# Nineteen loads on Pool's queue in joined packets, and an order table redrawn to match: a chunk-select attention with a gated feed-forward on one Trainium2 core

## The chip, the cores and the metric

The kernel runs on one core of one Trainium2 chip. The metric is the device time of one execution in microseconds (us). The profile comes from one profiled execution; its span is the time from the first to the last recorded instruction of the core. The engines are named as in the profile: PE is the matmul engine, DVE the vector engine, ACT the scalar engine, POOL is GpSimd, SP is the engine that does nothing here but issue DMAs.

## The reference

```python
B, H, S, D = 4, 8, 768, 64              # q, k, v
k_chunks = k.reshape(B, H, 24, 32, D)
k_min, k_max = min(k_chunks, axis=3), max(k_chunks, axis=3)
ub = sum(maximum(q * k_min, q * k_max), axis=-1)   # a bound for each query and chunk of 32 keys
ub = where(chunk is not later than the query's, ub, -1e9)
top_chunks = argsort(ub)[..., -6:]
scores = where(key's chunk in top_chunks and key <= query, q @ k.T / 8, -1e9)
attn = softmax(scores)
x = (attn @ v).transpose(0, 2, 1, 3).reshape(3072, 512)
gate = sigmoid(x @ w_gate)              # 512 -> 1536
return (gate * (x @ w_val)) @ w_out     # 1536 -> 512
```

All inputs and the output are float32.

## The kernel before

**Units.** The 3072 tokens are cut into blocks of 128 (six to a batch) and the blocks into eight units of up to 384 tokens: u0 holds the first blocks of batches 0, 1 and 2, whose queries see only their own block and so need no choice of chunks; u1 holds blocks 1 to 3 of batch 0; u2 blocks 4 and 5 of batch 0 and the first block of batch 3; u3 to u7 follow through batches 1 to 3. For each unit: queries and keys are transposed (kT, qT, kt, qf), chunk minima and maxima are made (kx0, kx1, in `L561`), the bounds are multiplied out on PE (ub), the six best are found (mx, ap, apt on DVE), queries and keys are laid out in halves with the mask of chosen chunks as extra rows (hq, hk, hqm; copies of `L346` on Pool or `L342` on ACT), scores (sc) go by PE to PSUM, ACT exponentiates (exp, `L859`), Pool masks diagonal blocks (cm, `L865`), PE multiplies by the values (pv, `L881`), DVE divides (rz, x), PE transposes (xps) and the feed-forward follows: g and v (`L931`), sigmoid by tanh on ACT, hg on DVE (`L943`), o (`L962`), a copy to SBUF (osb) and a store (out). Units 0 to 3 run it plainly; u4 with u5 and u6 with u7 run it in pairs, by a scheme with seven products for eight.

**Loads.** `load_first` loads a batch's first block: keys kf0_b and kf1_b and queries qf0_b and qf1_b (128 KB each, rows of 256 bytes) and values vf_b (256 KB). `load_wide` loads keys and queries of u1 and u2 by pairs of heads (k0_u1 to q3_u2; 192 and 128 KB). `load_v` loads the values of one block (v_b_i, 256 KB, rows of 256 bytes). `load_blocks` (`L537`) loads the keys and queries of batches 1 to 3 in four quarters each (k00_b, k01_b, k10_b, k11_b; 384 KB each, rows of 128 bytes). `weights` and `weights_out` load w_gate, w_val and w_out in three parts each (wg, wv, wo, 512 KB), by Pool's queue. All else but one store is issued by SP. The casts of batch 1's keys to half precision (k16_1_0 to k16_1_3) each need all four quarters.

**Order.** Nothing is scheduled at run time, nor by a planner at build time. The table `ORDER` (lines 94 to 270) holds 1893 words, one for each operation of the plan, in the order of emission. A word is the operation's name, after a colon the numbers of the buffer slots that it takes, and after an @ the engine, where that isn't the first of those that the operation allows. Each engine runs its operations in the order of the table and waits where one of them isn't ready. A slot whose old contents are still needed makes its next writer wait too: scores and gate products rotate through eight PSUM slots, batch loads through two large slots ("big") and values through six ("v").

```python
def load_v(b, ib, prio):
    t = raw_v[b, ib] = Buf("v", f"v_{b}_{ib}", [128, H, D])
    plan.add(f"v_{b}_{ib}", {SP: (450, 450)}, lambda e: nc.sync.dma_start(
        at(t), v[b, :, 128 * ib:128 * ib + 128].rearrange("h p d -> p h d")),
        writes=[t], prio=prio, dma=(1150, 256))
```

The pair of numbers after an engine and the `dma` values are costs from which the table was drawn elsewhere; they don't act when the kernel is built.

Of the kernel before, what the change touches and what calls it, by code (L numbers as in the profile page):

```python
# [94 lines left out]
tri0 ap1 ident epat0:0 ident16 tri k2_u1:0 kn_u1_2:0 kT_u1_2:0 kt_u1_2:0 q1_u2:1 vf1_1:1 epat kcr0 kx0_u1_2  # L95
qn_u2_1@DVE:2 k1_u2 k3_u1 kf1_0:0 q0_u1 qn_u1_0@DVE:3 qT_u1_0:1 qf_u1_0@DVE:0 kx1_u1_2:0 k1_u1 kn_u1_3:4 hkp001@ACT
kT_u1_3:2 q2_u2 hkp010@ACT qf0_0:1 qn_u2_2:5 hkp100@ACT q2_u1 qT_u2_1:3 scm_0:4,5 hkp101@POOL kn_u1_1@POOL:6 kT_u1_1:6
kt_u1_3:1 kx0_u1_3 kx1_u1_1 hq0 hkp000 k0_u1 kn_u1_0@POOL:0 kT_u1_0:7 kt_u1_0@DVE:2 q1_u1 qn_u1_1@POOL:3 qf0_1:2
hq1_u1_0 qf_u2_1:1 hq0_u2_1@POOL qT_u1_1:0 qf1_0 kf0_0 qf_u1_1@DVE q3_u1 kf1_2:3 kfT_0:1 kf16_0@DVE:4 hk0_u1_3@ACT
hk1_u1_3@ACT kx1_u1_3 kx0_u1_1 qfT_0:3 qn_u1_2:2 qf16_0:6 kt_u1_1:1 hk0_u1_2@POOL hkp110@POOL qT_u2_2:0 qn_u1_3@POOL:0  # L100
qT_u1_3:2 qf_u1_3 kn_u2_1:3 vf_1:4 vc_1 qT_u1_2:3 hkf1 hk1_u1_1@POOL hkf0@DVE kx0_u1_0 qm_u1_1:0 kx1_u1_0 kf0_2 qf1_1
kf1_1:5 kfT_2:6 kf0_1 qf0_3:0 qf_u1_2 qm_u1_3@ACT hk0_u1_1@ACT qf1_2:1 qf0_2 hk0_u1_0@POOL vf_2:4 qf_u2_2 vf_0:3 kfT_1:2
kxf1:1 scf_0:1 kf16_2:5 expf_0_0 qfT_1:3 kf16_1@DVE:0 kcr1 kxf0 hkp011 qfT_2:7 scm_1:0,2 qm_u1_0@POOL qf16_1:2 scf_1:2
qm_u1_2@ACT kcr_u1@POOL v10 qf16_2:4 v16_0_0 expf_1_1:3 expf_1_0 hkp111@ACT q3_u2 kcr_f ub_u1:6,4 ubn0_u1:0 ubm0_u1
kf1_3:5 ubn1_u1 k2_u2 qf1_3 pvf_1_1:1 pvf_0_0:3 kT_u2_1:7 mx0_u1:0 pvf_1_0:2 ap0_u1 qfT_3:0 rzf_0_0:0 k0_u2 wg0
hq1_u1_2@POOL wv0 apt0_u1:0 rzf_1_1:1 xf_0_0:0 hk1_u1_0@ACT kn_u2_2:6 qf16_3:0 hq0_u1_1 expf_0_1:1 kT_u2_2:6 kx0_u2_2
hq0_u1_0@POOL vf1_2:2 k3_u2 hq0_u1_2@POOL scm_2:4,0 scf_2:2 expf_2_1:0 hqm0_u1_0 vc_2 xpsf_0_0:5,0 xf_1_1:1 rzf_1_0:0
pvf_0_1:3 rzf_0_1:1 qn_u2_3@POOL:3 xf_1_0:2 q0_u2 sc_u1_0_1:0,1 hqm0_u1_2 expf_2_0 vf1_3:1 xpsf_1_1:1 xTf_1_1 pvf_2_0:4
qn_u2_0:6 xTf_0_0@ACT xpsf_1_0:2 rzf_2_0:0 xTf_1_0 xf_2_0:0 qT_u2_0:5 qf_u2_0@DVE kt_u2_2@DVE:1 kx1_u2_1:0
kn_u2_0@POOL:4 hq0_u1_3@POOL hq1_u1_3@POOL kt_u2_1@DVE:2 hk1_u1_2@POOL qm_u2_1@ACT:0 exp_u1_0_1 sc_u1_1_2:1,3 xpsf_2_0:4  # L110
exp_u1_1_2 xTf_2_0@ACT qT_u2_3:0 qf_u2_3 sc_u1_1_0:2 pvf_2_1:1 rzf_2_1:0 sc_u1_0_0:5 exp_u1_1_0 sc_u1_2_2:4,2 xf_2_1:1
hk1_u2_2@POOL exp_u1_2_2 xf_0_1:2 sc_u1_3_1:0,0 exp_u1_3_1 sc_u1_3_2:2 sc_u1_2_0:4 xpsf_2_1:1 sc_u1_3_0:0 exp_u1_0_0
exp_u1_3_0 v_0_2:2 kf0_3 hk0_u2_2@ACT xTf_2_1 qm_u2_2 ubm1_u1 kx1_u2_2 kn_u2_3@POOL:5 hk0_u2_1@POOL v16_0_2 xpsf_0_1:3
kT_u2_3:5 v_0_3:1 v_0_1:3 wg1 xTf_0_1 sc_u1_0_2:1 ap0 kT_u2_0:0 sc_u1_2_1:6 sc_u1_1_1:3 exp_u1_2_0 exp_u1_1_1 kx0_u2_1
wv1 cm_u1_1 v16_0_1 kx0_u2_0 v16_0_3 exp_u1_2_1 g_u0_0:4,0,0 exp_u1_0_2 tanh_u0_0 kfT_3:7 v_u0_0:3 mx1_u1 kx0_u2_3
ap1_u1 apt1_u1 exp_u1_3_2 kf16_3:6 kt_u2_3@DVE:0 g_u0_1:6,1,1 qm_u2_0@ACT tanh_u0_1 v_u0_1:1 vf_3:0 g_u0_2:4,2,2
v_u0_2:2 hqm1_u1_0@ACT qm_u2_3@ACT hq1_u1_1 pv_u1_1:7 kx1_u2_3 cm_u1_0 pv_u1_0 tanh_u0_2 hq1 sc_u1_4_1:5,3 k11_1:0
hqm1_u1_2 cm_u1_3 exp_u1_4_1 hk1_u2_3@ACT sc_u1_7_0:6,1 g_u0_3:4,3,3 sc_u1_7_2:5 exp_u1_7_0 exp_u1_7_2 wo2 hg_u0_0
hg_u0_1 rz_u1_0:0 x_u1_0:0 kx1_u2_0 cm_u1_2 sc_u1_4_0:3 hg_u0_2 pv_u1_3:1 sc_u1_7_1:7 pv_u1_2 sc_u1_6_2:2,0
sc_u1_5_1:6,2 hq0_u2_3@POOL k01_1 kt_u2_0@DVE:1 rz_u1_1:1 tanh_u0_3 sc_u1_4_2:0 cm_u1_7 kcr_u2@POOL wg2 exp_u1_4_2  # L120
sc_u1_5_2:5 v_u0_3:4 sc_u1_5_0:0 exp_u1_7_1 exp_u1_6_2 exp_u1_5_2 exp_u1_4_0 x_u1_1:1 g_u0_4:1,0,4 sc_u1_6_1:7 ub_u2:2,5
hg_u0_3 xps_u1_0:4,1 ubn0_u2:0 cm_u1_4 wv2 ubn1_u2 mx0_u2:0 ap0_u2 apt0_u2:0 hqm0_u2_2@DVE mx1_u2 pv_u1_4:3 exp_u1_5_0
v_u0_4:0 g_u0_5:2,1,5 wo0 hq0_u2_2@POOL cm_u1_5 vc_3 k00_1 k10_1 hk0_u2_3@ACT exp_u1_6_1 exp_u1_5_1 xT_u1_0@ACT
tanh_u0_4 hg_u0_4 tanh_u0_5 scf_3:7,6,3 pv_u1_7:5 sc_u1_6_0:4 exp_u1_6_0 cm_u1_6 v_u0_5:1 hg_u0_5 g_u0_6:2,2,6 expf_3_0
tanh_u0_6 v_u0_6:4 sc_u2_2_1:7,1 pv_u1_5 xps_u1_1:2 exp_u2_2_1 sc_u2_3_1:0,2 pv_u1_6 exp_u2_3_1 hk0_u2_0@POOL hqm0_u2_0
cmf_3_0 wo1 hg_u0_6 g_u0_7:1,3,7 rz_u1_3:0 sc_u2_2_2:7 sc_u2_2_0:4 expf_3_1:0 tanh_u0_7 exp_u2_2_2 rz_u1_2:1 x_u1_3:2
pvf_3_0:0 v_u0_7:5 g_u0_8:6,0,8 x_u1_2:0 rzf_3_0:0 xf_3_0:1 sc_u2_1_1:1,3 tanh_u0_8 sc_u2_3_0:3 exp_u2_3_0 xps_u1_2:7
exp_u2_2_0 hq0_u2_0 cmf_3_1 v_u0_8:0 g_u0_9:6,1,9 tanh_u0_9 v_u0_9:3 hk1_u2_0@POOL ap1_u2 xT_u1_1 hg_u0_8 cm_u2_3
g_u0_10:2,2,10 v_u0_10:4 hq1_u2_1 g_u0_11:0,0,11 v_u0_11:6 xT_u1_2 tanh_u0_10 xpsf_3_0:7,0 hg_u0_7 apt1_u2 hg_u0_9
pvf_3_1:5 rzf_3_1:1 hg_u0_10 tanh_u0_11 sc_u2_0_2:3,0 o0_u0_0:2,0 exp_u2_0_2 sc_u2_0_1:0 o1_u0_0 hq1_u2_3@POOL  # L130
xTf_3_0@ACT hg_u0_11 xps_u1_3:4 sc_u2_1_0:3 exp_u2_1_0 hqm1_u2_0@ACT hqm1_u2_2@ACT k16_1_0:3 o2_u0_0 o0_u0_1:7,1
xT_u1_3@ACT sc_u2_3_2:6 exp_u2_3_2 o1_u0_1 xf_3_1:0 osb_u0_0@DVE hq1_u2_0@DVE o2_u0_1 hq1_u2_2 hk1_u2_1@POOL osb_u0_1
v_0_4:4 exp_u2_0_1 out_u0_0 xpsf_3_1:3 kx0_1_0 xTf_3_1 cm_u2_1 v16_0_4 sc_u2_1_2:2 sc_u2_0_0:5 exp_u2_0_0 exp_u2_1_2
exp_u2_1_1 o0_u0_2:4,0 o1_u0_2 cm_u2_0 o2_u0_2 g_u1_0:6,3,12 osb_u0_2 tanh_u1_0 v_0_5:2 v16_0_5 cm_u2_2 kx0_1_3
pv_u2_2:3 kx1_1_3:1 kx1_1_0 sc_u2_6_2:7,1 pv_u2_1:0 pv_u2_3 sc_u2_7_0:5,3 kx1_1_2 kx0_1_2 sc_u2_7_2:2 sc_u2_5_0:1,2
exp_u2_7_0 k16_1_2@DVE:2 rz_u2_1:0 pv_u2_0 rz_u2_0:1 x_u2_1:1 exp_u2_6_2 sc_u2_4_2:4,0 exp_u2_7_2 exp_u2_4_2 x_u2_0:2
k16_1_1:5 kt_1_2:4 v11 q01_1:1 v_u1_0:6 g_u1_1:5,1,13 q11_1 k16_1_3@DVE:0 hg_u1_0 sc_u2_4_0:7 exp_u2_5_0 sc_u2_6_0:3
exp_u2_6_0 v_u1_1:2 xps_u2_1:0 xps_u2_0:4 g_u1_2:1,2,14 exp_u2_4_0 xT_u2_1@ACT q10_1 kx0_1_1 kx1_1_1 hk0_1_2 cm_u2_5
cm_u2_7 tanh_u1_2 tanh_u1_1 xT_u2_0@ACT hg_u1_1 v_u1_2:3 sc_u2_5_2:6 sc_u2_6_1:7 sc_u2_7_1:0 hg_u1_2 exp_u2_5_2 kt_1_0:6
sc_u2_5_1:1 exp_u2_6_1 exp_u2_7_1 g_u1_3:5,0,15 sc_u2_4_1:4 v_u1_3:2 g_u1_4:6,3,16 tanh_u1_3 cm_u2_4 exp_u2_5_1  # L140
tanh_u1_4 cm_u2_6 kcr_1@POOL hk0_1_0 q00_1 qf0_u3_2:0 qf0_u3_1 qf0_u3_3 hq0_u3_2@POOL qm_u3_2@ACT:0 v_u1_4:3
g_u1_5:7,1,17 v_u1_5:0 v_1_3:5 v_1_4:3 v_1_0:1 v16_1_3 v16_1_0 g_u1_6:5,2,0 qf0_u3_0 kt_1_1:1 hk1_1_1 qf0_u4_3:1
qm_u3_0@ACT tanh_u1_6 ub_u3:1,6 kt_1_3:2 hg_u1_3 exp_u2_4_1 tanh_u1_5 hq1_u3_2@POOL hk0_1_1 v_u1_6:5 g_u1_7:4,0,1
pv_u2_6:2 tanh_u1_7 hk1_1_2@ACT hg_u1_4 ubn0_u3:0 qf0_u4_1 ubm0_u3 pv_u2_5:7 mx0_u3:0 hg_u1_5 ap0_u3 qf0_u4_2 hk1_1_3
hg_u1_6 apt0_u3:0 hqm0_u3_0@DVE v_u1_7:3 g_u1_8:1,3,2 v_u1_8:4 hq0_u3_0@ACT tanh_u1_8 pv_u2_7 hg_u1_7 ubn1_u3
g_u1_9:0,1,3 qf0_u4_0 sc_u3_0_1:5,1 sc_u3_1_0:1,2 sc_u3_0_2:3 pv_u2_4 sc_u3_1_2:6 tanh_u1_9 hqm0_u3_2 rz_u2_3:0 ubm1_u3
v_1_1:0 out_u0_2 exp_u3_1_0 exp_u3_0_2 exp_u3_0_1 x_u2_3:0 v_u1_9:0 v16_1_1 v16_1_4 g_u1_10:1,2,4 v_u1_10:2 sc_u3_0_0:3
tanh_u1_10 g_u1_11:5,0,5 rz_u2_2:1 hg_u1_8 k01_2:0 v_1_2:4 k00_2 k11_2 k10_2 hg_u1_9 xps_u2_3:4 x_u2_2:1 sc_u3_2_0:0,3
xps_u2_2:7 sc_u3_1_1:1 q10_2:1 out_u0_1 mx1_u3 ap1_u3 apt1_u3 xT_u2_3 kx1_2_1:0 exp_u3_0_0 exp_u3_1_2 kx1_2_0 v_u1_11:3
# [1072 lines left out]
```

## Time and profile before

| | |
|---|---|
| median of 3 runs | 287.46 us (287.25 to 287.63) |
| the profiled execution | 287.56 us |
| its span | 285.8 us |
| granted clock of PE (mean) | 0.998 |
| PE busy | 268.1 us, 94% |
| DVE busy | 230.8 us, 81% |
| ACT busy | 213.2 us, 75% |
| POOL busy | 120.7 us, 42% |
| packets of SP's and ACT's loads and stores (q1, with q10) | 118592, 27.54 MB |
| packets of Pool's queue (q0) | 4752, 4.72 MB |

Busy time says how long an engine had work in hand, and an engine with idle time may still set the end if the idle time lies where others wait for it. The slices of the page are fortieths of the span, 7.1 us each, and a digit is the busy share in tenths. A row of groups gives line, engine and operation, out<-in, the count, then busy time, the mean of one in ns, and after the second bar the idle time in front with what ended it. A row of DMA issues gives the size and the median time from issue to landing.

### The profile page before, as it was taken

The page shows a single profiled execution, that of the slowest core. Times are in us where ns is not written, and L with a number is a line of the kernel's source. Part 1 is how long each engine was busy: PE and PEld are TensorE (multiplying, and loading weights), DVE is VectorE, ACT ScalarE, POOL GpSimd, SP SyncE. Part 2 cuts the span into 40 slices and gives each one's busy share as a digit, 9 for nine tenths or more (in the row PEclk, how much of TensorE's full clock was granted, in tenths as well). Part 3 has the DMA queues.
Part 4 walks back from the last instruction along what each step waited for, and adds up shares of the span by engine and source line. Part 5 has one row for each costly group of instructions (what it writes and reads, how often), then busy time and mean ns, then how long its engine had stood idle before and what let it go on. Part 6 is the DMA issues. An engine that isn't in the chain of part 4 may idle for free.

```text
span 285.8 us, 7062 instructions
## 1 busy us (share of the span) xinstructions
PE 268.1 (94%) x2626; PEld 170.8 (60%) x2626; DVE 230.8 (81%) x626; ACT 213.2 (75%) x452; POOL 120.7 (42%) x199
## 2 busy tenths in 40 slices
PE   1677899999999899999999999999999999999995
...
DMA  6999999999999999998031000100000020100005
GB/s 167 278 225 204 208 209 209 212 174 197 181 214 148 212 214 214 217 181 149 30 85 74 4 2 0 39 37 2 38 3 2 0 110 2 73 37 3 0 17 204
DMA packets 123377, 32.69 MB, mean 114 GB/s; under 512 B 111440, under 2 KB 120400, under 8 KB 123344
## 3 DMA queue, kind: packets, MB, share of 16 engines
...
q0 software_dynamic: 4752, 4.72, 10.2%
q8 instruction: 20, 0.33, 0.5%
...
q10 hardware_dynamic: 144, 0.07, 0.1%
...
## 4 chain that ended last, share of the span: by engine, by line
PE 74%; DMA 5%; SPq 4%; DVE 3%; ACT 3%; issue 1%; POOL 0%; DVEq 0%
PE o_u L962 19%; PE sc_u L848 10%; PE v_u L931 8%; PE g_u L931 8%; PE pv_u L881 6%; SPq L537 3%; PE sug_u6u L1041 3%; PE suv_u6u L1041 3%; PE sug_u4u L1041 3%; PE suv_u4u L1041 3%; DMA k<-in_k_dram 2%; DMA q<-in_q_dram 2%; PE ube_u L787 2%; PE xps_u L908 1%; PE srv_u6u L1041 1%; PE srg_u6u L1041 1%
## 5 line engine op out<-in xcount | busy, mean ns | idle before, releaser
L859 ACT ACTIVATE att_u<-sc_u 128x512 f16<-128x512 f32 (+3 forms) x184 | 91.4, 556 | 16.2 <-PE sc_u L848 15.0
L962 PE MATMUL o_u<-wo,hg_u 128*128 128x512 f16 x216 | 52.8, 379 | 0.0
L865 POOL TENSOR_SCALAR_AFFINE_SELECT att_u<-att_u 128x384 f16<-128x384 f16 (+1 forms) x56 | 29.1, 529 | 48.7 <-ACT att_u L859 45.8
L931 PE MATMUL v_u<-xT_u,wv 128*128 128x384 f16 x192 | 39.1, 326 | 0.0
L931 PE MATMUL g_u<-xT_u,wg 128*128 128x384 f16 x192 | 39.0, 326 | 0.0
L962 PEld LDWEIGHTS <-hg_u 128*128 128x128 f16 x216 | 20.4, 98 | 20.1 <-issue 0.6
L939 ACT ACTIVATE gate_u<-g_u 128x384 f16<-128x384 f32 x48 | 23.7, 498 | 8.7 <-PE g_u L931 8.5
L943 DVE SCALAR_TENSOR_TENSOR hg_u<-gate_u,v_u 128x384 f16<-128x384 f16 x48 | 25.3, 539 | 5.6 <-PE v_u L931 2.3
L848 PE MATMUL sc_u<-hqe,hke 128*128 128x128 f16 (+2 forms) x220 | 28.7, 243 | 1.2 <-DVE kx_u L561 0.9
L848 PE MATMUL sc_u<-hqo,hko 128*128 128x128 f16 (+2 forms) x220 | 27.6, 243 | 0.5 <-DVE hg_u L943 0.5
L881 PE MATMUL pv_u<-v,att_u 128*128 128x65 f16 x640 | 27.3, 193 | 0.7 <-POOL att_u L865 0.6
L881 PEld LDWEIGHTS <-att_u 128*128 128x128 f16 x640 | 24.7, 98 | 4.9 <-POOL att_u L865 1.1
L931 PEld LDWEIGHTS <-wv 128*128 128x128 f16 x192 | 17.8, 98 | 10.5 <-issue 0.5
L931 PEld LDWEIGHTS <-wg 128*128 128x128 f16 x192 | 18.0, 98 | 10.0
L848 PEld LDWEIGHTS <-hke 128*128 128x128 f16 x220 | 16.7, 98 | 6.8 <-issue 1.6
L848 PEld LDWEIGHTS <-hko 128*128 128x128 f16 x220 | 16.8, 98 | 6.3 <-ACT att_u L859 0.6
L971 ACT ACTIVATE osb_u<-o_u 128x512 f32<-128x512 f32 x17 | 10.1, 606 | 9.3 <-PE o_u L962 9.3
L962 PE MATMUL o_u<-wo,hgp_u 128*128 128x512 f16 (+1 forms) x72 | 17.0, 370 | 0.0
L553 POOL CAST v<-v 128x512 f16<-128x512 f32 x23 | 13.8, 611 | 4.1 <-DMA v<-in_v_dram 3.8
L900 DVE TENSOR_TENSOR x_u<-pv_u,rz_u 128x384 f16<-128x384 f32 (+1 forms) x28 | 14.6, 528 | 0.7 <-PE xps_u L908 0.3
L342 ACT COPY xT_u<-xps_u 128x384 f16<-128x384 f16 (+1 forms) x22 | 10.1, 474 | 5.2 <-PE xps_u L908 5.1
L346 POOL CAST k<-k 128x768 f16<-128x768 f32 x9 | 7.5, 833 | 13.9 <-DMA k<-in_k_dram 13.8
(215 smaller groups left out, 597.3 us busy)
## 6 DMA issues: line engine op xcount, KB each, us to landing
v<-in_v_dram SPq DMA_DIRECT2D x23, 256.0 KB, 4.5
out_dram<-osb_u SPq DMA_DIRECT2D x23, 256.0 KB, 2.1
...
wg<-in_moe_w_gate_dram POOLq DMA_DIRECT2D x3, 512.0 KB, 8.9
wv<-in_moe_w_val_dram POOLq DMA_DIRECT2D x3, 512.0 KB, 10.0
wo<-in_moe_w_out_dram POOLq DMA_DIRECT2D x3, 512.0 KB, 9.1
...
```

Source lines behind the costliest of these rows:

```text
L342: nc.scalar.copy(o, i)
L553: plan.add(f"v16_{b}_{ib}", {POOL: pool(H * D)}, lambda e: nc.gpsimd.tensor_copy(v16[b % 2][:, ib, :, 0:D], at(t)), reads=[t], writes=[("v ...
L848: nc.tensor.matmul(at(t)[:, o:o + 128 * m], hk[b % 2][e_][:, p, 128 * jb:128 * jb + 128], hq[u.side][e_][:, p, 128 * x:128 * (x + m)], sta ...
L859: plan.add(f"exp_{u.name}_{h}_{y}", {ACT: act(n)}, lambda e, t=t, att=att, b0=b0, n=n: nc.scalar.activation(at(att)[:, b0:b0 + n], at(t), ...
L865: nc.gpsimd.affine_select(out=dv, in_=dv, compare_op=ALU.is_ge, fill=0.0, base=0, pattern=[[0, u.m], [1, 128]], channel_multiplier=-1)
L881: nc.tensor.matmul(at(pv)[:, last, x, :], at(att)[:, c:c + 128], v16[b % 2][:, jb, h, :], start=(jb == 0), stop=(jb == ib))
L900: plan.add(f"x_{u.name}_{p}", {DVE: dve(u.t)}, lambda e: nc.vector.tensor_tensor(at(x_).rearrange("p a (e d) -> p e a d", e=2), at(pv)[:, ...
L931: nc.tensor.matmul(at(t), w16[:, c, 128 * fb:128 * fb + 128], at(u.xt)[:, c, :], start=(c == 0), stop=(c == 3))
L939: plan.add(f"tanh_{u.name}_{fb}", {ACT: act(T)}, lambda e, g=g, gate=gate: nc.scalar.activation(at(gate), at(g), AF.Tanh, scale=0.5), read ...
L943: plan.add(f"hg_{u.name}_{fb}", {DVE: dve(T)}, lambda e, w_=w_, gate=gate, hg=hg: nc.vector.scalar_tensor_tensor(at(hg), at(gate), 1.0, at ...
L962: nc.tensor.matmul(at(o), hgs[c][1][1]()[:, 128 * tb:128 * tb + 128], wo16[:, fc, lo:hi], start=(c == 0), stop=(c == NFB - 1))
L1041: nc.tensor.matmul(at(t), left[i](c), right[i](c), start=first and c == 0, stop=c == 1, skip_group_check=not first)
```

## The change

First, a helper `read` issues a load by the engine that its word names: SP as before, or Pool, with the option `single_packet`, which joins the rows that one DMA engine moves for this load into one packet. The loads of `load_first`, `load_wide` and `load_v` are allowed both engines; `load_blocks` isn't.

```diff
+    def read(e, o, i):
+        if e == SP:
+            nc.sync.dma_start(o, i)
+        else:
+            nc.gpsimd.dma_start(o, i, single_packet=True)
+
     def load_first(b, prio):
...
-                plan.add(f"{n}f_{b}", {SP: (550, 550)}, lambda e, t=t[n], src=src: nc.sync.dma_start(
+                plan.add(f"{n}f_{b}", {SP: (550, 550), POOL: (930, 930)}, lambda e, t=t[n], src=src: read(e, 
                     at(t), src[b, :, 0:128].rearrange("h s d -> s h d")),
...
-                    plan.add(f"{n}f{e_}_{b}", {SP: (550, 550)}, lambda e, t=t[n], src=src, e_=e_: nc.sync.dma_start(
+                    plan.add(f"{n}f{e_}_{b}", {SP: (550, 550), POOL: (750, 750)}, lambda e, t=t[n], src=src, e_=e_: read(e, 
...
     def load_wide(u, prio):
...
-                plan.add(f"{'kq'[j]}{p}_{u.name}", {SP: (450, 450)}, lambda e, j=j, p=p, src=src: nc.sync.dma_start(
+                plan.add(f"{'kq'[j]}{p}_{u.name}", {SP: (450, 450), POOL: (800, 800)}, lambda e, j=j, p=p, src=src: read(e, 
...
     def load_v(b, ib, prio):
-        plan.add(f"v_{b}_{ib}", {SP: (450, 450)}, lambda e: nc.sync.dma_start(
+        plan.add(f"v_{b}_{ib}", {SP: (450, 450), POOL: (930, 930)}, lambda e: read(e, 
             at(t), v[b, :, 128 * ib:128 * ib + 128].rearrange("h p d -> p h d")),
```

Second, the whole table is another: the same 1893 operations in another order, with other slots, and 174 of them on another engine. Nineteen of these are loads that go from SP to Pool, in this order: k3_u1, k0_u1, qf0_1, qf1_1, qf1_2, q0_u2, kf0_2, q3_u2, v_0_2, vf_3, v_0_5, v_0_4, v_2_4, v_1_3, v_1_1, v_2_5, v_3_1, v_3_5, v_3_3. The keys and queries of batch 3's first block (kf0_3 to qf1_3) stay with SP. The other moves between engines are copies and shuffles: 84 between ACT and DVE, 35 from Pool to ACT, 19 from ACT to Pool, 13 from Pool to DVE and 3 back, and one store.

Around the places that the prediction speaks of the order runs like this (loads only, * for Pool's queue, from the first batch-1 quarter to the last batch-2 quarter of keys; then Pool's own operations, then DVE's):

```
before, loads: k11_1 wo2* k01_1 wg2* wv2* wo0* k00_1 k10_1 wo1* v_0_4 out_u0_0 v_0_5 q01_1 q11_1 q10_1 q00_1
               v_1_3 v_1_4 v_1_0 v_1_1 out_u0_2 k01_2 v_1_2 k00_2 k11_2 k10_2
after, loads:  k01_1 k10_1 wo1* wg1* wg2* vf_3* k00_1 k11_1 v_0_5* wv2* wo0* wo2* v_0_4* q10_1 q01_1 v_2_4* q00_1 q11_1
               v_1_3* v_1_2 out_u0_0 out_u0_1 k00_2 v_1_1* k10_2 v_1_0 k01_2 k11_2
before, Pool:  hq1_u2_3 k16_1_0 hk1_u2_1 cm_u2_1 v16_0_4 cm_u2_0 v16_0_5 cm_u2_2
after, Pool:   v_0_4* cm_u2_0 cm_u2_3 v_2_4* v16_0_4 k16_1_0 hq1_u2_3 v_1_3* hqm1_u2_2 cm_u2_1 cm_u2_5
after, DVE:    hg_u1_5 hg_u1_4 hg_u1_6 kx0_2_1 mx1_u3 kx0_2_3 rz_u2_3 x_u2_3 ap1_u3 apt1_u3 hg_u1_7 kx0_2_2
```

At the end, the last token block of u7 is stored in two parts, 384 and 128 columns wide. Before, the narrow part comes last (osbb_u7_2 on ACT, outb_u7_2 from ACT's queue); after, the wide part does (osb_u7_2 on DVE, out_u7_2 from ACT's queue). Lines behind the helper move down by six.

More of the change, by code (lines that the diff above doesn't have):

```diff
@@ L94 @@
 ORDER = """
[L95 to L149, printed above, removed]
@@ L265 @@
[L265 to L269 removed]
+hq1 vf1_2:0 ident v10 ident16 k2_u1:0 kn_u1_2:1 kT_u1_2:0 epat0:0 q1_u2:1 qn_u2_1@DVE:2 k3_u1@POOL k2_u2 kf1_0:0 kf0_1:1
@@ new lines @@
+kt_u1_0@DVE:2 qn_u1_2:5 kf0_2@POOL qm_u1_1@ACT:0 qn_u1_3:4 kx1_u1_3 kt_u1_1@DVE:0 scm_0:2,5 q2_u2 vf1_1:6 vc_1 kx0_u1_3
+kxf1:1 kcr_f kf1_3:5 kf16_1:3 qT_u1_2:4 qf_u1_2 qfT_1:3 qf16_1@DVE:1 qT_u1_3:6 qfT_0:7 qf0_3 hk0_u1_1@POOL hk1_u1_0@POOL
+qf16_0@DVE:5 hq0_u1_1 q3_u2@POOL hk0_u1_0@ACT qf_u1_3 hq1_u1_0@DVE kx1_u1_0 qm_u1_3 scm_1:4,3 scf_1:1 scf_0:2 qfT_2:6
+qm_u1_2@ACT expf_1_0 expf_0_0 kx0_u1_0 hkp000 kcr_u1@POOL qm_u1_0@ACT expf_0_1:3 expf_1_1:0 qf16_2:4 kx1_u2_2:1
+v_0_2@POOL:2 pvf_0_0:7 hq0 rzf_0_0:0 wg0 wv0 kn_u2_3@POOL:1 kfT_2:4 pvf_1_0:2 rzf_1_0:1 ap0 kf0_3 vf_2:0 ub_u1:0,5
```

289 lines of the change are left out of this document (169 added, 120 removed).

## Prediction

> **What bounds the kernel now.** I read the page first: busy shares, the slices, the queues, the issues.
>
> ```profile
> PE 268.1 (94%) x2626; PEld 170.8 (60%) x2626; DVE 230.8 (81%) x626; ACT 213.2 (75%) x452; POOL 120.7 (42%) x199
> PE   1677899999999899999999999999999999999995
> DMA  6999999999999999998031000100000020100005
> ...
> v<-in_v_dram SPq DMA_DIRECT2D x23, 256.0 KB, 4.5
> ...
> wg<-in_moe_w_gate_dram POOLq DMA_DIRECT2D x3, 512.0 KB, 8.9
> wv<-in_moe_w_val_dram POOLq DMA_DIRECT2D x3, 512.0 KB, 10.0
> ```
>
> TensorE is at nine tenths nearly everywhere; the DMA engines are full for the first 18 slices (some 130 us), then nearly empty. So the loads can matter only in the first half. Next the table by stretches (us, busy time and count for each engine, granted clock, DMA share, GB/s):
>
> ```profile
> 0.00:20.00 20.00, 10.08 (x64) 7.65 (x65) 12.03 (x28) 14.70 (x25) 12.70 (x25) 1.00 0.88 221
> 20.00:40.00 20.00, 16.97 (x196) 10.85 (x196) 16.20 (x67) 18.39 (x43) 15.62 (x30) 1.00 1.14 209
> 60.00:70.00 10.00, 10.00 (x103) 6.26 (x101) 7.34 (x13) 7.40 (x16) 4.58 (x9) 1.00 1.12 206
> 86.00:96.00 10.00, 8.82 (x87) 5.64 (x85) 7.56 (x27) 7.56 (x18) 4.87 (x8) 1.00 1.02 175
> 96.00:282.00 186.00, 185.94 (x1806) 117.03 (x1803) 158.95 (x410) 138.86 (x298) 62.32 (x93) 1.00 0.29 67
> 282.00:285.80 3.80, 0.36 (x7) 0.19 (x4) 0.36 (x1) 0.28 (x1) 0.00 (x0) 0.88 0.50 184
> ```
>
> TensorE has no work for 9.9 + 3.0 us in the first 40, for 1.2 us between 86 and 96, and, at the very end, for 3.4. Elsewhere it is full, at full clock. Both kernels issue the same matmuls, so the time after is this work plus those holes, changed, plus new ones. The chain of waits shows what makes the 1.2 us (start, length, what):
>
> ```profile
> 84.97 7.02 DMA k<-in_k_dram
> ...
> 93.08 0.94 DVE kx L561
> 94.02 0.45 DVE hg_u L943
> ...
> 94.51 0.32 PE sc_u L848
> ```
>
> Batch 2's last quarter of keys lands at 84.97 + 7.02 = 91.99; VectorE, which works in written order, holds a gate product (hg) behind the chunk bounds (kx) of those keys, and TensorE's next scores need the accumulator that hg empties.
>
> **The change part by part.** *The 19 issues on Pool.* The nearest rows are weight issues:
>
> ```profile
> L492 POOL DMA_DIRECT2D wg<-in_moe_w_gate_dram x3 | 2.5, 841 | 0.0
> L493 POOL DMA_DIRECT2D wv<-in_moe_w_val_dram x3 | 2.3, 754 | 0.0
> ```
>
> Their mean is (841 + 754) / 2 = 798 ns, so 19 add 15.2 us to Pool's 120.7. Nine of them (7.2 us) come before the first gate matmul; Pool is idle for 20 − 12.70 + 20 − 15.62 = 11.7 us of those 40. ScalarE is the tighter one there: 18.39 of 20 busy between 20 and 40, and the new table gives it shuffles and query copies that Pool did. I cost this at nothing because Pool's idle time covers it; without that cover, up to the 2.0 us or so by which 7.2 and ScalarE's extra work would overfill 20 to 40. For a gain the bound is the DMA share of 0.88 in the first 20 us: more packets in flight can at best fill the other 12%, 2.4 us. I take 0, with ends −2.4 and +2.0.
>
> *Less work ahead of the first gate matmul.* The first gate matmul now has two transposed key groups and two score groups less before it; at the 0.16 us from start to start of a score group (67.95 − 67.79 in rows below), 4 × 0.16 = 0.65 us of work moves from the holes of the start into the full stretch: **+0.7**.
>
> *What a joined load costs the DMA engines.* No row has one. Between 60 and 70 us unjoined loads moved 206 GB/s at a share of 1.12, 184 GB/s for a full share: 262144 B / 184 = 1.42 us for a 256 KB load. At the end, large output packets moved 184 GB/s at 0.50, 368 for a full share: 0.71 us. I take 0.71 for a joined load, the row for long packets, and keep 1.42 for the range. [...]
>
> *The wait at 66 us.* Rows of before around it, keys by their tile, then Pool and TensorE in order of time:
>
> ```profile
> L537 SPq DMA_DIRECT2D k<-in_k_dram x4: 1431/6047/12317, 33.4 to 55.2; - x4
> DMA to landing us min/median/max: 7.5/16.4/24.2
> 62.94 0.82 POOL L346 CAST k<-k 128x768 f16<-128x768 f32 x1 [8.68 <-DMA k<-in_k_dram]
> 63.83 0.40 POOL L346 COPY hko<-kt_u 64x256 f16<-64x256 f16 x1
> 64.30 0.41 POOL L865 TENSOR_SCALAR_AFFINE_SELECT att_u<-att_u 128x256 f16<-128x256 f16 x1
> 64.22 2.75 PE L962 MATMUL o_u<-wo,hg_u 128*128 128x512 f16 x12
> 66.81 0.81 PE L931 MATMUL g_u<-xT_u,wg 128*128 128x384 f16 x4
> 67.46 0.49 PE L881 MATMUL pv_u<-v,att_u 128*128 128x65 f16 x11
> 67.79 0.33 PE L848 MATMUL sc_u<-hqo,hko 128*128 128x256 f16 x2
> 67.95 0.83 PE L881 MATMUL pv_u<-v,att_u 128*128 128x65 f16 x22
> 68.62 0.55 PE L848 MATMUL sc_u<-hqo,hko 128*128 128x128 f16 x5
> ```
>
> Pool sat idle 8.68 us for the last quarter of batch 1's keys (issued at 55.2, landed 7.5 later: 62.7), cast them at 62.94 and masked block pair 1 of unit u2 (cm_u2_1) at 64.30; TensorE reached that pair (pv_u2_1) at 67.95, 3.2 us behind the mask's end. The new table turns this round. TensorE reaches pv_u2_1 earlier: the output projection (66.81 − 64.22 = 2.59), a gate group (67.46 − 66.81 = 0.65) and a score group (0.16) go behind it, 3.40 us; two value products (68.62 − 67.95 = 0.67) and four score groups (4 × 0.16 = 0.64) come ahead. Net 2.09, so 65.9, and 66.6 with the 0.7 above. And Pool reaches the mask later: k16_1_0, the cast that needs all four quarters, then a query shuffle of 0.40, the issue of v_1_3 (0.80), a second shuffle (hqm1_u2_2; hqe rows of that form below), the mask (0.41).
>
> ```profile
> L346 POOL COPY hqe<-apt_u 64x640 f16<-64x640 f16 x3 | 2.3, 769 | 0.7 <-DVE apt_u L821 0.6
> ```
>
> From landing to mask's end: 0.24 + 0.82 + 0.40 + 0.80 + 0.77 + 0.41 = 3.4 us. The landing moves too: v_0_4 and v_0_5, which were issued behind these keys, now run beside them from Pool's queue: 2 × 0.71 later, 64.1. The mask ends at 64.1 + 3.4 = 67.5 and TensorE loses 67.5 − 66.6 = 0.9, with 0.1 until its weights are loaded **+1.0**. Ends: 0 (landing as before) and, when three loads (v_2_4 as well) cost 1.42 each, 62.7 + 4.3 + 3.4 − 66.6 = 3.8. Queued behind the cast on Pool are also the masks and casts after it.
>
> *The wait at 92 us.* In before 29.3 us lie between the last landings of batch 1's and batch 2's keys; the new tables put three unjoined v loads less between (3 × 1.42 = 4.3) and join two more (2 × 0.71 = 1.4): 64.1 + 29.3 − 4.3 − 1.4 = 87.7. But more VectorE work now stands between those keys and the gate product that TensorE needs (hg_u1_7):
>
> ```profile
> 87.81 0.42 DVE L900 TENSOR_TENSOR x_u<-pv_u,rz_u 128x256 f16<-128x256 f32 x1
> 88.15 0.81 DVE L810 MAX8 mx_u<-ubn_u 128x8 f32<-128x8 f32 x10
> 88.99 0.32 DVE L815 TENSOR_TENSOR ap<-ubn_u,mx_u 128x160 f16<-128x160 f32 x1
> 89.35 0.51 DVE L821 STREAM_TRANSPOSE apt_u<-ap 128x320 f16<-128x320 f16 x1
> 92.18 1.84 DVE L561 TRANSPOSE_TENSOR_REDUCE kx<-k 128x24 f32<-128x768 f32 x2 [2.15 <-DMA k<-in_k_dram]
> 85.98 0.49 PE L881 MATMUL pv_u<-v,att_u 128*128 128x65 f16 x11
> ```
>
> Two bounds 1.84, top-8 search 0.84, comparison 0.36, transpose 0.51, a reciprocal and x 0.5, hg 0.45: 4.5 us, so hg ends at 92.2. The scores waiting for it (sc_u3_0_2) started just before the value product at 85.98; 2.8 us of other matmuls go ahead of them now (two groups of 0.65, a value product of 0.33, seven small ones of 0.16), so TensorE arrives at 85.9 + 2.8 + 0.7 + 1.0 = 90.4 and waits 1.8 where it waited 1.2: **+0.6**, with ends −1.2 (hg in time) and, with both landings 2.9 late but TensorE late as well, +2.1.
>
> *The end.* The last store was 64 KB behind a ScalarE copy of 128 columns; now it is 192 KB behind a VectorE copy of 384:
>
> ```profile
> 282.40 0.28 ACT osb_u L971
> L972 DVE TENSOR_SCALAR osb_u<-o_u 128x512 f32<-128x512 f32 x6 | 4.1, 690 | 6.8 <-PE o_u L962 6.8
> out_dram<-osb_u SPq DMA_DIRECT2D x1, 192.0 KB, 2.0
> out_dram<-osb_u ACTq DMA_DIRECT2D x1, 64.0 KB, 1.9
> ```
>
> 690 × 3/4 is about 0.55 against 0.28, plus 2.0 against 1.9: **+0.4**, with the ends 0.1 and 0.5. After 96 us TensorE is idle for 0.06 of 186 us, and the joined v loads there (v_2_5 to v_3_3) land well ahead; I cost them at nothing.
>
> Sum: 287.56 (the profiled run: span 285.8 and 1.8 around it) + 0.7 + 1.0 + 0.6 + 0.4 = 290.3; that run is 0.1 above the median of the three, so 290.2.
>
> **The rivals.** *Faster: the loads do come sooner.* Two issuing queues fill the start's DMA engines (−2.4) and k_1 and k_2 are early enough that no mask waits and the wait at 92 goes (−1.2): 287.5 + 0.7 + 0.4 − 2.4 − 1.2 = 285.0; with half of the start's gain 286.2. For it: the DMA row is full and short packets fill it. Against: TensorE's start hangs on transposes and shuffles as well, and Pool's order puts a wait on k_1 ahead of a mask.
>
> *The joining saves nothing.* Packets stay as costly as SP's, which would be the change not doing what its helper says. Then the landing at 66 us is 62.7 + 2.8 and up to 4.3 later, the hole there 2.3 to 3.8, the one at 92 up to 2.1 more: 287.5 + 0.7 + 3.0 + 1.5 + 0.4 = 293.1.
>
> *Loads by Pool land late.* The only loads there took 8.9 to 10.0 us to land, v loads by SP 4.5. If that is the queue and not their size, a query piece such as q3_u2 lands 5.5 us late; ScalarE's next in order (qn_u2_3) waits for it, its idle time of 20 − 18.39 = 1.6 absorbs that much, and 3.9 us go to the exponentials and TensorE: 290.2 + 3.9 = 294.1. It decides from about 1.6 us of lateness. Against: the weights are twice as large. [...]
>
> **How the numbers follow.** Forecast as summed (288 to 292) 0.46; joining saves nothing 0.13; late by Pool 0.09; faster 0.27; within 0.2%, which is about what a measurement of this kernel can tell from no change, 0.05. Slower: 0.46 + 0.13 + 0.09 = 0.68. Range 285.5 to 295.0: from half to all of the start's gain at the low side to the late case and 0.9 at the high side; the forecast's own range is 288 to 292.
>
> **What would show it.** The forecast is right if the chain of waits has Pool's mask (L871 after the shift of lines) ahead of a value product near 67 us with the key cast before it, if TensorE's busy time in 86 to 100 us is under that stretch by 1.5 to 2, and if the span's last piece is a VectorE copy. It is wrong if the first gate matmul starts over 1 us away from 33 us, if batch 1's last keys land by 62.7, if Pool's issues of joined loads take far from 798 ns, or if TensorE has holes of over 1 us after 100 us.

## The result and the profile after

| | before | after |
|---|---|---|
| median (runs) | 286.82 us (20, 285.26 to 288.20) | 289.18 us (20, 286.87 to 291.39) |
| ratio | | 1.0069, interval 1.0049 to 1.0090 |
| the profiled execution, its span | 287.56, 285.8 us | 291.39, 289.7 us |

The changed kernel is slower: by 0.7% in the ratio, by 2.4 us between the medians. Its times spread over 4.5 us where the old kernel's spread over 2.9. Its profiled execution is the longest of its twenty, and the ratio leaves it out; the first experiment has a profile from the other end of the spread, and the two are read side by side.

The table by stretches of after (columns as in the prediction):

```profile
0.00:20.00 20.00, 11.73 (x80) 8.78 (x80) 15.53 (x33) 16.84 (x28) 13.97 (x28) 1.00 0.91 238
20.00:40.00 20.00, 13.53 (x153) 8.94 (x150) 15.41 (x66) 16.73 (x41) 13.11 (x22) 0.99 1.24 214
40.00:60.00 20.00, 19.16 (x207) 13.13 (x208) 10.23 (x38) 13.32 (x32) 13.04 (x25) 0.84 1.26 199
60.00:70.00 10.00, 10.00 (x99) 6.47 (x98) 8.75 (x15) 7.37 (x17) 6.24 (x10) 1.00 1.06 189
86.00:96.00 10.00, 10.00 (x101) 6.91 (x100) 9.62 (x30) 9.55 (x20) 7.87 (x12) 1.00 1.12 203
96.00:282.00 186.00, 186.00 (x1819) 117.65 (x1817) 157.87 (x418) 143.09 (x302) 62.99 (x87) 1.00 0.26 60
```

TensorE is idle 1.65 us less than before in the first 20 us (8.27 against 9.92), 3.4 us more in the next 20 (6.47 against 3.03), and runs at a mean clock of 0.84 in the 20 after that. Where the forecast had two waits, at 66 and 92 us, TensorE is full. The chain of waits names the place (start, length, what):

```profile
21.98 16.30 DMA v<-in_v_dram
38.28 0.06 issue
38.34 0.61 POOL v L559
38.94 0.67 POOL hqo L346
...
40.25 0.53 POOL att_u L871
40.78 0.05 issue
40.83 1.11 PE pv_u L887 x17
```

This is v_0_3, a value load that *stayed* with SP: issued at 21.98, landed 16.30 us later. Pool casts it, and behind that cast in Pool's order stand two shuffles and the mask that the second value product needs. On TensorE (start, length, count, and in brackets the idle time in front):

```profile
30.35 0.81 PE L937 MATMUL g_u<-xT_u,wg 128*128 128x384 f16 x4
...
35.84 0.40 PE L887 MATMUL pv_u<-v,att_u 128*128 128x65 f16 x8
39.00 0.22 PE L887 MATMUL pv_u<-v,att_u 128*128 128x65 f16 x2 [2.75 <-POOL v L559]
40.83 1.11 PE L887 MATMUL pv_u<-v,att_u 128*128 128x65 f16 x17 [1.61 <-POOL att_u L871]
```

The first gate matmul starts at 30.35, 2.65 us earlier than the 33.00 of before. Then the hole, 2.75 + 1.61 us, more than takes it back. And the hole has a tail, seen in stretches of 2 us (the third number from the end is the granted clock):

```profile
36.00:38.00 2.00, 0.24 (x9) 0.15 (x5) 1.09 (x3) 1.65 (x4) 0.00 (x0) 1.00 1.39 214
38.00:40.00 2.00, 0.22 (x2) 0.10 (x1) 0.00 (x0) 0.00 (x0) 1.60 (x3) 0.92 1.45 217
40.00:42.00 2.00, 1.18 (x19) 1.11 (x20) 0.48 (x2) 0.00 (x0) 1.90 (x5) 0.50 0.95 146
42.00:44.00 2.00, 2.00 (x10) 1.07 (x9) 0.27 (x1) 0.66 (x2) 1.89 (x5) 0.50 0.73 84
44.00:46.00 2.00, 2.00 (x23) 1.83 (x22) 0.20 (x1) 1.21 (x3) 1.61 (x3) 0.50 1.39 205
46.00:48.00 2.00, 2.00 (x39) 1.23 (x42) 1.11 (x2) 1.18 (x4) 0.52 (x1) 0.88 1.27 259
```

After 3.4 us in which TensorE is busy for 0.22 (36.26 to 39.67) the granted clock falls to 0.50; TensorE comes back at it and keeps it until 5.7 us after it is busy again (40.83 to 46.49). Four gate matmuls then take 1.28 us from start to start (42.16 to 43.44) where they take 0.65 at full clock. Between 40 and 46 us TensorE is busy for 5.18 us at half clock, so an estimated 2.6 us are lost there; its busy time in the whole span is 2.0 us above before's (270.2 for 268.1).

### The profile page after: what moved, and what is told of

Read it like the earlier page. It is cut to its first block, busy times and chain, and to the rows that moved or that the text cites. A ratio compares the mean times of both kernels' runs of the same rounds, so it can differ in the third digit from the quotient of the medians.

```text
span 289.7 us, 7086 instructions
## 1 busy us (share of the span) xinstructions
PE 270.2 (93%) x2626; PEld 173.4 (60%) x2626; DVE 233.7 (81%) x638; ACT 221.6 (77%) x466; POOL 125.3 (43%) x192
## 4 chain that ended last, share of the span: by engine, by line
PE 84%; DMA 6%; ACT 5%; POOL 2%; DVE 2%; issue 0%; POOLq 0%; DVEq 0%
PE o_u L968 21%; PE sc_u L854 12%; PE g_u L937 10%; PE v_u L937 10%; PE pv_u L887 7%; DMA v<-in_v_dram 6%; PE sug_u4u L1047 3%; PE suv_u6u L1047 3%; PE sug_u6u L1047 3%; PE suv_u4u L1047 3%; PE ube_u L793 2%; ACT hko L342 2%; PE xps_u L914 2%; PE srv_u4u L1047 1%; PE srv_u6u L1047 1%; PE srg_u6u L1047 1%
## 5 line engine op out<-in xcount | busy, mean ns | idle before, releaser
L871 POOL TENSOR_SCALAR_AFFINE_SELECT att_u<-att_u 128x384 f16<-128x384 f16 (+1 forms) x56 | 31.4, 572 | 49.5 <-ACT att_u L865 46.9
L937 PE MATMUL g_u<-xT_u,wg 128*128 128x384 f16 x192 | 39.7, 330 | 0.0
L887 PE MATMUL pv_u<-v,att_u 128*128 128x65 f16 x640 | 28.3, 195 | 4.4 <-POOL v L559 2.8
L887 PEld LDWEIGHTS <-att_u 128*128 128x128 f16 x640 | 25.9, 99 | 9.0 <-issue 3.0
L854 PE MATMUL sc_u<-hqo,hko 128*128 128x128 f16 (+2 forms) x220 | 27.7, 251 | 0.0
L854 PE MATMUL sc_u<-hqe,hke 128*128 128x128 f16 (+2 forms) x220 | 26.5, 243 | 0.3 <-ACT hke L342 0.2
L945 ACT ACTIVATE gate_u<-g_u 128x384 f16<-128x384 f32 x48 | 23.5, 501 | 4.1 <-PE g_u L937 3.8
L937 PEld LDWEIGHTS <-wg 128*128 128x128 f16 x192 | 18.1, 99 | 10.9 <-issue 0.9
L559 POOL CAST v<-v 128x512 f16<-128x512 f32 x23 | 14.8, 648 | 12.0 <-DMA v<-in_v_dram 11.6
L977 ACT ACTIVATE osb_u<-o_u 128x512 f32<-128x512 f32 x19 | 11.4, 600 | 9.0 <-PE o_u L968 7.8
L904 DVE RECIPROCAL rz_u<-pv_u 128x6 f32<-128x6 f32 (+1 forms) x28 | 5.0, 180 | 11.9 <-PE pv_u L887 11.8
L1047 PEld LDWEIGHTS <-Sv 128*128 128x128 f16 x96 | 9.0, 98 | 6.1
```

The costliest lines, as they stand in the source:

```text
L559: plan.add(f"v16_{b}_{ib}", {POOL: pool(H * D)}, lambda e: nc.gpsimd.tensor_copy(v16[b % 2][:, ib, :, 0:D], at(t)), reads=[t], writes=[("v ...
L854: nc.tensor.matmul(at(t)[:, o:o + 128 * m], hk[b % 2][e_][:, p, 128 * jb:128 * jb + 128], hq[u.side][e_][:, p, 128 * x:128 * (x + m)], sta ...
L871: nc.gpsimd.affine_select(out=dv, in_=dv, compare_op=ALU.is_ge, fill=0.0, base=0, pattern=[[0, u.m], [1, 128]], channel_multiplier=-1)
L887: nc.tensor.matmul(at(pv)[:, last, x, :], at(att)[:, c:c + 128], v16[b % 2][:, jb, h, :], start=(jb == 0), stop=(jb == ib))
L937: nc.tensor.matmul(at(t), w16[:, c, 128 * fb:128 * fb + 128], at(u.xt)[:, c, :], start=(c == 0), stop=(c == 3))
L945: plan.add(f"tanh_{u.name}_{fb}", {ACT: act(T)}, lambda e, g=g, gate=gate: nc.scalar.activation(at(gate), at(g), AF.Tanh, scale=0.5), read ...
```

## The experiments

Theory A: the loss is value loads that SP moves in rows of 256 B beside weights that Pool moves in packets of about 1 KB. Theory B: the half clock is all of it. Theory C: the order of the computing work costs, not the queues. Theory D: loads issued by Pool come too late in a table not drawn for them.

**e1: the changed kernel again.** No edit.

> The changed kernel once more, for a profile at full clock and more times. Theory A (one value load is starved): in the first profile TensorE started the first gate matmul at 30.35 us, 2.65 earlier than before, and then stood still for 4.7 us between 36 and 41 because v_0_3 landed 16.3 us after its issue; so every run shows that hole at 3 to 5 us, and the time is 288 to 290 us. Theory B (the half clock between 40 and 46 us in that profile is what costs): a run at full clock has the same hole and is within 0.5 us of before.

287.49 us median (12 runs, 284.92 to 290.73); ratio to before 1.0037 (1.0006 to 1.0068). Its profiled execution took 285.49 us and has no hole at 36 us:

```profile
20.00:40.00 20.00, 16.94 (x210) 11.87 (x208) 17.46 (x71) 18.80 (x48) 18.37 (x31) 1.00 1.28 221
86.00:96.00 10.00, 9.19 (x76) 5.36 (x75) 9.87 (x20) 8.43 (x18) 5.35 (x8) 1.00 0.96 168
```

"Every run shows the hole" is thus wrong. B is wrong too: the mean granted clock of every run is on record, and the runs at 0.998 or more (8 of these 12, and 13 of the 20 above) have medians of 287.14 and 288.86 us, against 285.71 for such runs of before beside e1. The changed kernel is slower at full clock as well. Of the 20 runs above, the profiled one alone had a mean clock as low as 0.987, so its pair of hole and half clock is not what the others show.

The tile's view tells the two executions apart (SP's value loads between 20 and 46 us of after, then 20 to 36 us of e1: first and last issue, then issue to landing, min/median/max):

```profile
L507 SPq DMA_DIRECT2D v<-in_v_dram x2: 407/817/1227, 21.5 to 22.0; - x2
DMA to landing us min/median/max: 10.2/13.3/16.3
```

```profile
L507 SPq DMA_DIRECT2D v<-in_v_dram x2: 402/458/515, 20.9 to 21.4; - x2
DMA to landing us min/median/max: 4.2/6.7/9.2
```

Half a microsecond decides. Pool issues wg0 at 21.25 us in after, ahead of v_0_1 and v_0_3 (21.46 and 21.98); in e1 at 21.56, behind both (20.88 and 21.39). The five profiles in which SP issues v_0_3 within 1 us of wg0 line up (e2, e5 and e6 come below):

| | e2 | e1 | e5 | e6 | after |
|---|---|---|---|---|---|
| issue of v_0_3 after that of wg0, us | −0.65 | −0.17 | −0.05 | −0.01 | +0.73 |
| v_0_3 from issue to landing, us | 4.5 | 9.2 | 10.2 | 12.2 | 16.3 |

In these five, the later v_0_3 is issued the longer it takes to land, from 4.5 to 16.3 us. The queues of after between 27 and 34 us (queue, packets, MB, share of the DMA engines; q0 is Pool's, q1 SP's):

```profile
q0 software_dynamic: 1105, 1.10, 92.2%
q1 hardware_dynamic: 1072, 0.27, 29.1%
```

In these 7 us the two queues moved nearly as many packets; in bytes SP's moved a quarter of Pool's, with rows of 256 B beside packets of 1 KB.

With the start's gain kept, e1 does show the forecast's second wait. On DVE, in order (the last operations before hg_u1_7), and on PE:

```profile
82.78 0.98 DVE L567 TRANSPOSE_TENSOR_REDUCE kcr<-k 128x24 f32<-128x768 f32 x1 [0.91 <-DMA k<-in_k_dram]
83.68 0.77 DVE L816 MAX8 mx_u<-ubn_u 128x8 f32<-128x8 f32 x10
...
86.92 0.52 DVE L949 SCALAR_TENSOR_TENSOR hg_u<-gate_u,v_u 128x384 f16<-128x384 f16 x1
```

```profile
87.49 0.27 PE L854 MATMUL sc_u<-hqe,hke 128*128 128x256 f16 x1 [0.41 <-DVE hg_u L949]
```

From the landing to hg's end are 87.44 − 82.78 = 4.7 us, for 4.5 forecast; but TensorE loses only 0.8 in that stretch (10 − 9.19) against 1.2 before.

**e2: the loads not joined.**

```diff
-            nc.gpsimd.dma_start(o, i, single_packet=True)
+            nc.gpsimd.dma_start(o, i)
```

> The changed kernel with the nineteen Pool loads not joined (the option left out). Theory A: rows of 256 B become packets again (Pool's queue from 6048 packets to some 20000), the first gate matmul comes 0.5 to 1.5 us later, the hole behind v_0_3 stays; 289 to 291 us. Rival (joining is worth nothing here): within 0.3 us of the changed kernel.

288.51 us median (12 runs, 285.46 to 291.24), ratio 1.0057 (1.0024 to 1.0089): not told apart from e1 by these intervals. The first gate matmul starts at 30.65 us, as in e1 (30.66). The queue rows of after and of e2 say why:

```profile
q1 hardware_dynamic: 103664, 23.21, 38.9%
q0 software_dynamic: 6048, 8.78, 14.9%
```

```profile
q1 hardware_dynamic: 103664, 23.21, 39.8%
q0 software_dynamic: 6048, 8.78, 14.6%
```

Before, q0 had 4752 packets with 4.72 MB. The nineteen loads thus travel in 1296 packets of 3.1 KB in the mean, with the option or without; the forecast of some 20000 packets was wrong. The joining comes with Pool's queue, and in these records the option adds nothing. Nor is it one packet for each DMA engine and load: in after's trace a value load of 256 KB by Pool goes in packets of 4096 bytes, which is 64 of them for 16 engines.

**e3: the nineteen loads back on SP, the new table kept** (nineteen words lose their @POOL).

> The changed kernel's table with the nineteen loads given back to SP at the same words. Theory A: the start loses what the second queue gave (first gate matmul at 32 to 33 us), v_0_3 still lands late because the weights wv1 and wo1 still run ahead of it; 290 to 293 us. Rival C (the order of the computing work is what costs, not the queues): within 0.5 us of the changed kernel.

298.62 us (6 runs, 297.67 to 299.65), ratio 1.0425 (1.0390 to 1.0460): worse than theory A said, and theory C's "no difference" is refuted. The first gate matmul starts at 32.02 us. TensorE's waits between 20 and 64 us:

```profile
PE pvf L657 <- POOL vf L346: 3.5, 1, 3.5
PE kT_u L692 <- POOL kn_u L346: 2.1, 1, 2.1
PE pv_u L887 <- POOL att_u L871: 1.6, 1, 1.6
```

The chain there has two value loads of 14.93 and 9.40 us, on SP beside the weights. The mean clock is 0.974 to 0.983 in every run, and 0.50 from 42 to 44 and from 64 to 68 us of the profile, so part of the loss is half clock.

**e4: the old table, with only the nineteen loads on Pool** (the helper is taken over, nineteen words get @POOL).

> The old table with only the nineteen words sent to Pool's queue and joined. Theory A: wv1 and wo1 stay behind v_0_3, so no hole at 36 us; a small gain or nothing at the start: 285 to 287 us. Rival D (issues by Pool stand behind its shuffles and come too late in a table not drawn for them): TensorE idles more in the first 60 us and the time is 288 to 291 us.

318.58 us (6 runs, 316.71 to 319.18), ratio 1.1106 (1.1066 to 1.1147). Theory D has the sign right, and is too small by a factor of six (32.8 us where it said at most 5): in the first 70 us TensorE waits 7.0 us at one place in a row of query transposes, 6.8 us in three waits for copies of keys, 3.1 and 2.6 at others, and the mean clock is 0.946 to 0.957 in every run. So neither half of the change stands alone: the new table needs Pool's queue, and Pool's queue needs the new table.

**e5: two weight issues later.** On Pool, wv1 goes behind wg1, wo1 behind wg2.

```diff
-kx1_u2_3 wv1 hqm0_u1_0 ... exp_u1_0_1 wo1 hk1_u1_1@POOL ... wg1 ... wg2
+kx1_u2_3 hqm0_u1_0 ... exp_u1_0_1 hk1_u1_1@POOL ... wg1 wv1 ... wg2 wo1
```

> The changed kernel with two words moved: the issue of wv1 goes behind wg1's and that of wo1 behind wg2's on Pool's queue, so that only wg0 and wv0 run beside v_0_1 and v_0_3. Theory A (v_0_3 is starved by weights that nobody needs yet): v_0_3 lands by 34 us, TensorE has no hole of over 1 us between 34 and 42 us in any profile, 285 to 286.5 us and a spread of under 3 us where the changed kernel spreads over 5. Rival C (the order of the computing work costs): as the changed kernel, 287 to 289 us.

287.66 us (12 runs, 285.30 to 289.95), ratio 1.0040 (1.0013 to 1.0068). There is no hole behind v_0_3 in its profile, but no gain in the median and no smaller spread: as an explanation of the whole loss, "weights that nobody needs yet" is wrong. The waits of TensorE from 28 to 100 us:

```profile
PE g_u L937 <- ACT osb_u L977: 0.9, 1, 0.9
...
PE pv_u L887 <- DVE hg_u L949: 0.4, 1, 0.4
```

The first is new: a copy of an output block on ACT, at 73.38 us, waits 2.50 us for its buffer, that is for the landing of a store which SP issued among loads.

**e6: e5, and the last copy but one on ACT** (osb_u6_2@DVE becomes osb_u6_2@ACT).

> As the kernel with the weights later, and the copy osb_u6_2 ahead of the last one goes to ACT, which is idle by then, in place of DVE. Expected by the rows of the end: the last copy no longer stands behind the other on DVE (1.21 us for both), so from the last matmul to the end 3.9 to 4.0 us in place of 4.6, and 0.6 us less in all: 284.5 to 286 us. Rival: the store's own 2 us hide it, no difference.

287.15 us (12 runs, 285.67 to 288.86), ratio 1.0034 (1.0004 to 1.0065). From the last matmul's start to the end are 4.17 us; in after 4.25, in e1 4.26, before 3.63. The rival holds: freeing DVE gains under 0.1 us. The new wait of e5 is there again, with 1.8 us, and TensorE waits 1.1 us for wv0. Its profiled execution (288.27 us, full clock) is the one profile of a long run without half clock, though of a kernel next to the changed one: the time goes in such waits, not in one hole.

**e7: values first.** v_0_1 and v_0_3 go to Pool as well, ahead of wg0 and wv0.

```diff
-v_0_2@POOL:2 ... wg0 wv0 kn_u2_3@POOL:1 kfT_2:4 ... v_0_1:3 v_0_3:1
+v_0_2@POOL:2 ... kn_u2_3@POOL:1 kfT_2:4 v_0_1@POOL:3 v_0_3@POOL:1 wg0 wv0
```

> The changed kernel with v_0_1 and v_0_3 issued by Pool as well, directly ahead of wg0 and wv0. Theory A: both land by 28 us, no hole at 36 us, the first weights some 2 us later and the first gate matmul at 31.5 to 32.5 us; 285.5 to 287 us with a spread of under 3 us. Rival C: 287 to 289 us.

285.96 us (12 runs, 285.59 to 287.20), ratio to before 1.0002 (0.9979 to 1.0025). As theory A says: the loads land at 28.1 and 28.9 us, the first gate matmul is at 31.47, and the spread falls from 5.8 us in e1 to 1.6. The order of the computing work is the changed kernel's, so C falls. But wg0 is also issued 2.0 us later than in e1 (23.56 for 21.56), which may spare SP's other loads too; e7 doesn't tell these two effects apart.

**e8: the first weights earlier.** wg0 and wv0 go ahead of kcr_u1 and v_0_2.

> The changed kernel with the issues of wg0 and wv0 moved ahead of v_0_2's and of kcr_u1 on Pool, some 1.5 to 2.5 us earlier: the bad case by force. Theory A: v_0_3 always lands behind the weights, at 37 us or later, the hole of 4 to 5 us and the stretch of half clock behind it are in every run: 290 to 293 us. Rival C: as the changed kernel, 287 to 289 us, or less because the weights come sooner.

289.76 us (4 runs, 288.84 to 289.84), ratio 1.0116 (1.0078 to 1.0154), each run at a mean clock of 0.986 to 0.988. Two stretches, then Pool and TensorE in order of time:

```profile
20.00:28.00 8.00, 4.00 (x66) 2.11 (x64) 5.69 (x28) 7.02 (x18) 1.89 (x3) 0.98 1.18 218
28.00:36.00 8.00, 5.39 (x46) 4.58 (x46) 4.36 (x16) 3.27 (x9) 5.82 (x11) 0.60 1.05 186
```

```profile
29.88 0.61 POOL L346 CAST vf<-vf 128x512 f16<-128x512 f32 x1 [7.80 <-DMA vf<-in_v_dram]
...
30.54 0.38 PE L657 MATMUL pvf<-vf,attf 128*128 128x65 f16 x4 [5.10 <-POOL vf L346]
```

A bad case is forced, hole and low clock in the one profile and the low clock in every run, but the load that starves is another than expected. Pool waits 7.80 us for vf_2, the values of batch 2's first block, which SP issued at 17.53 us and which took 12.3 us to land, for 4.0 in after; TensorE waits 5.10 us behind it. The keys of u2 (k0_u2, k1_u2) are as late, 12.0 and 8.8 us for 4.5 and 4.9 in after, and v_0_3 lands at 32.2 already. Here, as in after, the late loads are those that SP had issued about when the weights began.

**e9, e10, e11: can the change be made to gain?** e9 is e7 with e6's edit of the end; e10 is e9 with only v_0_3 ahead of wg0 and v_0_1 back on SP; e11 is e10 with e5's later weights.

> The values-first kernel (v_0_1 and v_0_3 by Pool ahead of wg0) with the last copy but one, osb_u6_2, on ACT. From the rows so far the two add: no hole behind the value loads, and 3.9 us from the last matmul to the end in place of 4.6: 285.0 to 285.6 us median, with a spread under 2.5 us, 0.2 to 0.4% below before. Rival: the end's gain is taken by another store, 285.9 us as without it.

> As the kernel before this one, but only v_0_3 goes to Pool ahead of wg0, v_0_1 stays with SP. wg0 and wv0 are then issued 0.9 us earlier, and in the values-first kernel TensorE waited 2.1 us at 30 to 35 us for wv0: 284.3 to 285.3 us. Rival: v_0_1 on SP now takes v_0_3's place and is starved in some executions: 285 to 289 us with a spread of over 3 us.

> As the run with one value load first, and wv1 and wo1 later as in the run with the weights later. That run lost up to 1.8 us at 70 to 76 us, where a store landed late and held a copy on ACT and with it TensorE's accumulator; if that comes from the shifted weights it shows again: 285 to 287 us. If it was one execution's accident, 284.3 to 285.3 us.

| | median (12 runs) | ratio to before |
|---|---|---|
| e9 | 285.85 us (285.60 to 286.73) | 0.9999 (0.9975 to 1.0023) |
| e10 | 285.98 us (285.21 to 288.51) | 1.0002 (0.9973 to 1.0031) |
| e11 | 285.79 us (285.12 to 290.44) | 0.9976 (0.9947 to 1.0005) |

The hole can be taken away, and then the changed kernel is level with the old one; none of the three is clear of it. The end's edit brings under 0.1 us again (3.79 us behind the last matmul's start, for 3.86 in e7). Moving one load instead of two brings its 0.8 us at the start, in e11's profile: the first gate matmul is at 30.65 there and the first value product of the feed-forward at 33.50, for 31.47 and 34.28 in e7. In e10's profile the first gate matmul is at 31.83, since TensorE ran at half clock from 27.7 to 31.1 us. The medians show none of it. The store's wait of e5 isn't in e11's profile, so the later weights alone don't bring it. The spread of e10 and e11 is wider than that of e9, so v_0_1 on SP may keep some of the risk; no profile shows one of their long runs.

## Why the prediction was right, and by which steps it was not

The forecast was 290.2 us, slower, with 288 to 292 as its own range; measured were 289.18 and, with other runs of before beside it, 287.49. Sign and size came out, by luck: the sum put the loss into two waits at 66 and 92 us, and the runs put it elsewhere. By the forecast's own signs it was wrong in two points, the first gate matmul over 1 us away from 33 us and batch 1's last keys landed before 62.7; and of what was to show it right only the VectorE copy at the end came.

*The issues on Pool and the start: mis-sized.* I took 0 with −2.4 as the best end; the first gate matmul came 2.65 us earlier in after and 2.3 in e1, and TensorE's idle time ahead of it fell from 12.9 us to 10.9 and 10.4. The DMA share in the first 20 us rose only from 0.88 to 0.91 and 0.93, but the bytes from 221 to 238 and 248 GB/s. The bound was misread: the same table has shares of 1.14 and 1.12, so 1.00 is no ceiling. Nor is the gain all the queue's: with all loads on SP (e3) the new order moves 236 GB/s in those 20 us, and that matmul comes 1.0 us earlier than before. Pool's issues of value loads took 0.89 to 0.96 us for 0.80. That less work stands ahead of the first gate matmul (+0.7) can't be told from TensorE's busy time, 20.06 us before, 19.47 in after and 20.27 in e1.

*A joined load at 0.71 us: about right.* The nineteen loads moved in packets of 3.1 KB in the mean. In after's trace a packet of 4096 bytes took 166 ns in the median and a row of 256 bytes by SP 18 ns, so a 256 KB load takes an estimated 0.66 us of each of the 16 DMA engines, against 1.15 in rows. That these come from the queue and not from the option was not foreseen. What joining alone saves can't be told from these runs, since none has unjoined loads on Pool's queue.

*The wait at 66 us: fell.* Pool's chain ran as forecast. In after the cast began at 66.53 and the mask of pv_u2_1 at 69.61, but TensorE came to that product at 71.36, being late itself. In e1 the keys landed at 60.34, the cast ran at 60.39, the mask began at 63.24, and TensorE reached pv_u2_1 at 64.24: half a microsecond to spare. The input that failed was the landing: 62.04 and 60.34 for a forecast 64.1.

*The wait at 92 us: the mechanism was right, its size not.* Shown in e1; it cost 0.8 us in place of 1.8, less than the 1.2 it replaced.

*The end: +0.6 for +0.4,* from 3.63 to 4.25 us behind the last matmul's start.

*What the forecast lacked* is the step that decides: the loads that the change leaves on SP. I asked what Pool's issues meet on Pool, and what Pool's landings hold up, but not what Pool's queue, filled with wv1 and wo1 before 28 us, does to SP's rows. Before's own trace had the row for it: its three value loads beside wg0 and wv0 (issued at 22.0, 23.5 and 24.3 us) took 8.3 to 11.5 us to land, where such loads took 4.0 in the median from 100 us on, with no weights in flight.

```profile
DMA to landing us min/median/max: 8.3/11.5/11.5
```

There the old table had room for it. The rival "loads by Pool land late" had the sides exchanged; Pool's value loads landed in 4.4 us in after, as SP's in 4.5 (medians). And I held the clock to be full throughout, which the profiled execution wasn't (0.50 from 39.67 to 46.49 us). The start's gain means little by itself: in after, e1, e2, e5 and e6 some or all of it is lost at a later place (36, 70 or 87 us), where a load or store sets the time.

In sums, against before's profile: after's holes up to 100 us are 1.4 us more in all (15.6 for 14.2), its busy time 2.0 more (the half clock), the end 0.6: 4.0, where the spans differ by 3.9. For e1 the holes are 11.5 for 14.2, and the end 0.6 more: −2.1, where the spans differ by −2.0 (283.8 against 285.8).

What is shown, then: in after's profile, a load on SP that moves beside weights (v_0_3, 16.3 us) makes the hole, and the clock of 0.50 comes behind it; e8 has such a pair in its profile and a mean clock of 0.986 to 0.988 in every run; and e7, with the two value loads ahead of the weights on Pool's queue, ends both the loss and the spread, while e5 shows that it is not only the two early weights. What stays open is where the ordinary runs of the changed kernel lose their time. Most of them ran at full clock, so not in a pair of hole and half clock as in the profiled one; that it is late loads on SP there too is argued from e7 and e6, and no profile shows it.
